# Feed-forward in three chunks of 768 tokens instead of four batches of 576, and a list schedule that no longer prefers the array shape in use

## The chip, the cores and the metric

The kernel runs on one core of one Trainium2 chip. The metric is the device time of one execution in microseconds (us); less is better. The engines are named as in the profile: PE is TensorE (matmuls), PEld its weight loads, DVE is VectorE, ACT is ScalarE, POOL is GpSimd, SP is SyncE, whose queue issues all the DMAs.

## The reference

Three layers follow one another on a batch of 4 with 576 tokens; the weights arrive as float64, the rest and the output are float32.

```python
# attention, 8 heads of 64, mask by blocks of 64 tokens
scores = scale * np.matmul(q, k.transpose(0, 1, 3, 2))
...
x = softmax(scores) @ v                      # (4, 576, 512)
# middle layer
theta = x @ w_theta
y = einsum('ts,bsd->btd', w_tok_r, x * cos(theta)) + einsum('ts,bsd->btd', w_tok_i, x * sin(theta))
u = x + y
x = u + np.maximum(u @ w_ch, 0.0)
# last layer
h = (x.transpose(0, 2, 1) @ U @ V).transpose(0, 2, 1)   # rank 32
u = x + h
out = u + np.maximum(u @ w_ch1, 0.0) @ w_ch2            # 512 -> 2048 -> 512
```

## The kernel before

**The whole program is planned on the host.** The code doesn't call the engines directly. It records every operation with a due time (`at_time`, `spread`, from the numbers in `CFG`), and `Line.run` then makes a list schedule: for each engine, in modelled time, it takes the ready operation with the lowest priority number (its due time, and in later rounds its latest start). `plan` repeats this `ROUNDS` times. The outcome is a fixed order of instructions on each engine; on the chip the engines wait for each other by semaphores alone. Tiles have tags, and a tag has homes (slots of SBUF or banks of PSUM); an operation whose tile finds no free home is passed over, and `LOOSE` says for which tags a later tile may overtake an earlier one.

**The choice on PE.** A matmul uses the array in a shape: 128 rows by 128 columns mostly, 64 by 128 for the scores (two heads at a time), 128 by 64 for the product with v. `Line.run` remembers the most urgent ready matmul, but if that one has another shape than the last one issued, it looks on, and takes the first one in its list that has the shape in use; only a candidate of a wrong shape ends the search, when it is due later than the first by more than `PATIENCE`, which is 0.

**Work in order.** 16 head pairs of attention (4 a batch); while they run, the weights of the middle layer are read and decoded from their float64 bits by ACT and DVE. Behind each four pairs comes the middle layer of that batch: `theta` (matmuls `th` of 512 columns), `sines`, `product`, `mix_r` and `mix_i` (token mix, tile `y`), `chan` (channel product, tile `c`), then `lowrank` and `expand`. `expand` writes u of the batch to DRAM (`u3d`). A matmul of float32 exactness is done as three matmuls of float32r parts: high with high, high with low, low with high (`three`, and loops like it).

**The feed-forward layer** takes the token columns of one batch in halves of 288 (`SH`), and uses a Strassen-Winograd scheme of 7 products for 2 by 2 blocks. Per batch and step j (8 steps of 256 hidden units):

- `make_u` reads u of the batch from `u3d` and splits it into two float32r parts (tile `uf`): for batch 1 into slots of the middle layer's `xT`, for the others into tag `U`.
- `ff1` makes four quarters of 12 matmuls (tile `m`, 288 columns), takes relu and the differences that the second product wants, seven pieces of h of 288 columns in all, and writes them to DRAM (`hd`) in four DMAs, three of them with two pieces.
- `ff2` reads them back (tile `hr`, tag `G`) in pairs of two pieces, splits them into float32r parts (tile `hv`, tag `U`, two pieces in one tile), and runs the products into eight PSUM banks (tile `acc`): s = 0 has four products, s = 1 three, each 2 x 3 matmuls. All eight steps j of s = 0 come first, then all of s = 1. `leave` then adds the banks and the residual u together (tiles `ea`, `eb`, `o`) and writes `outT`.

Tag `U` has 8 homes: four in SBUF space that attention gave up (`NU`), and four of the nine slots `T` that held the token weights. Tag `W` (weights w1 and w2 in parts) has the other five slots `T`, seven new ones (`NB`), and the slots of `w_theta` (`Kt`), `w_ch` (`Kc`) and U, V. A slot of `T` comes free for its second use when all tiles of that tag are done.

`EJ` is 5: the first five steps of batches 0 and 1 are due while the middle layer of batch 3 runs, the rest after it. The due times end with

```python
    late = [(b, j) for b in (0, 1) for j in range(EJ, NJ)] + [(b, j) for j in range(NJ) for b in (2, 3)]
    ...
    for b in range(B):
        for s in range(2):
            for j in range(NJ):
                at_time(t, ff2, b, s, j)
```

The operations are issued from one line at the very end of `build`, so nearly all rows of the profile carry that line, L1295; they are told apart by their tiles.

Of the kernel before, what the change touches and what calls it, by code (L numbers as in the profile page):

```python
# [45 lines left out]
CFG = dict(L=60., d0=0., d1=0.84, d2=1.0, dec=1.8, T=13.68, P=13.88, R=25.74, I=29.568, X=2.61, m0=4., m1=80., w1=1., w2=2., w3=0.2, u0=3., f1=150., f2=177., v0=0., v1=140.)  # L46
# [5 lines left out]
NB = 7  # L52
NRX = 5
NG = 7
NS_ = 4
INX = (1, 2, 6)
LONE = (2, 3)
NU = 4
UX = (1,)
EJ = 5  # L60
MIX = 0
NTW = 5
# [7 lines left out]
LOOSE = {"pm": 1, "pa": 1, "F": 3, "G": 6}  # L70
# [3 lines left out]
PATIENCE = 0.0  # L74
# [109 lines left out]
class Line:  # L184
# [143 lines left out]
    def fits(self, o):  # L328
        got = []
        for x in o.bufs:  # L330
            if x.home is not None or x.tag is None:
                continue
            free = [h for h in self.homes[x.tag] if h.since is not None and h not in [g for _, g in got]
                    and not any(self.left_of.get(a) for a in h.after[x.tag])]
            if not free:
                return None
            k = sum(y.tag == x.tag for y, _ in got)
            if x not in [y for _, _, y in self.order[x.tag][:k + 1]] and not len(free) > LOOSE.get(x.tag, 99):
                return None
            got.append((x, min(free, key=lambda h: h.since)))  # L340
        return got

    def run(self):
# [38 lines left out]
        while events:  # L382
# [18 lines left out]
            while c:  # L401
# [132 lines left out]
def build(tc, ctx, qT, kT, v, w_theta, wtokT, w_ch, U, V, w1, w2, outT):  # L534
# [38 lines left out]
    u3 = [dram.tile([DM, S], F32, name=f"u3d{b}") for b in range(B)]  # L573
    h3 = [[dram.tile([P, 7 * SH], F32, name=f"hd{b}_{j}") for j in range(NJ)] for b in range(B)]
# [60 lines left out]
    def abank(name):  # L635
        return line.tile([P, 512], F32, "pa", name, PSUM)

# [18 lines left out]
    u3d = [line.fixed(u, f"u3d{b}") for b, u in enumerate(u3)]  # L656
# [279 lines left out]
    def lowrank(b, i):  # L936
# [5 lines left out]
        xp = bank(f"xq{b}_{i}")  # L942
# [13 lines left out]
    def expand(b, d):  # L956
        gs_ = st[b]["Gs"]
        for g in range(2):
            gs = slice(g * SH, (g + 1) * SH)
            hp = bank(f"h{b}_{d}_{g}")  # L960
# [3 lines left out]
        nc.sync.dma_start(u3d[b][d * P:(d + 1) * P, :], xTs[b][:, d, 0:S])  # L964
# [34 lines left out]
    L = CFG["L"]  # L999
    for gp in range(NP):  # L1000
        spread(gp * L / NC4, (gp + 1) * L / NC4, pair_calls(gp))
# [5 lines left out]
    for b in range(B):  # L1007
        t0 = (b + 1) * L
# [15 lines left out]
    hd = [[line.fixed(h3[b][j], f"hd{b}_{j}") for j in range(NJ)] for b in range(B)]  # L1024
# [27 lines left out]

    def load_w1(f):
        t = line.tile([P, 2, DM], F32R, "W", f"w1_{f}")
# [9 lines left out]
    wparts, wv = {}, {}  # L1064

    def wpairs(j):
        q, k = divmod(j, 2)
        pair = [P, 2, 2, HW]
        if q in LONE:
            first = line.tile([P, 1, 2, HW], F32R, "W1", f"w2d{j}")  # L1070
        else:
            if q not in wparts:
                wparts[q] = line.tile(pair, F32R, "W", f"w2d{q}")
            first = wparts[q][:, k:k + 1]
# [31 lines left out]
    def make_u(b):  # L1106
        uu[b] = []
        for c in range(NC4):
            raw = rawslot(f"u3_{b}_{c}", F32)
            nc.sync.dma_start(raw, u3d[b][c * P:(c + 1) * P, :])  # L1110
            if b in UX:
                if c % 2 == 0:
                    x = xtile(f"uf{b}_{c}", [P, 2, 2, S], F32R)
                y = x[:, c % 2]
            else:
                y = line.tile([P, 2, S], F32R, "U", f"uf{b}_{c}")
            rnd("sh", y[:, 0], raw)
            sub(y[:, 1], raw, y[:, 0], "sl")
            uu[b].append(y)
# [4 lines left out]
    def fbank(name):  # L1124
        return line.tile([P, 512], F32, "F", name, PSUM)[:, :SH]
# [5 lines left out]
    def ff1(b, j):  # L1131
        n = f"{b}_{j}"
        ha, hb, hc, hdd = [halves(f"{x}{n}", tag="G") for x in ("ha", "hb", "hc", "hd")]

        def quarter(k, t):
            bank_ = fbank(f"m{n}_{k}{t}")
            w = w1t[2 * j + k]
            ts_ = slice(t * SH, (t + 1) * SH)
            for c in range(NC4):
                three(bank_, [w[g][:, c] for g in range(2)], [uu[b][c][:, g, ts_] for g in range(2)], c == 0, c == NC4 - 1)  # L1140
            return bank_

        relu(ha[:, 0], quarter(0, 0))
        relu(hc[:, 1], quarter(1, 1))
        m = quarter(0, 1)
        nc.vector.scalar_tensor_tensor(out=ha[:, 1], in0=m, scalar=0.0, in1=ha[:, 0], op0=ALU.max, op1=ALU.subtract)
        nc.sync.dma_start(hd[b][j][:, 0:2 * SH].rearrange("p (v c) -> p v c", v=2), ha)
        nc.vector.scalar_tensor_tensor(out=hb[:, 1], in0=m, scalar=0.0, in1=hc[:, 1], op0=ALU.max, op1=ALU.subtract)
        tt(hb[:, 0], hc[:, 1], ha[:, 1], ALU.subtract)
        nc.sync.dma_start(hd[b][j][:, 2 * SH:4 * SH].rearrange("p (v c) -> p v c", v=2), hb)  # L1150
        relu(hc[:, 0], quarter(1, 0))
        nc.sync.dma_start(hd[b][j][:, 4 * SH:6 * SH].rearrange("p (v c) -> p v c", v=2), hc)
        tt(hdd[:, 0], hc[:, 0], hb[:, 0], ALU.subtract)
        nc.sync.dma_start(hd[b][j][:, 6 * SH:], hdd[:, 0])
# [3 lines left out]
    def ff2(b, s, j):  # L1158
        w = wv[j]
        if s == 0:  # L1160
            group, at = FIRST4, ((0, 2, ("B11", "T1")), (2, 4, ("T2", "T3")))
        else:
            group, at = LAST3, ((4, 6, ("B21", "B22")), (6, 7, ("T4",)))
        v = {}
        for a, c, names in at:
            k = c - a
            raw = halves(f"hr{b}_{j}_{a}", n=k, tag="G")
            nc.sync.dma_start(raw, hd[b][j][:, a * SH:c * SH].rearrange("p (v c) -> p v c", v=k))
            t = line.tile([P, 2, 2, SH], F32R, "U", f"hv{b}_{j}_{a}")[:, :k]
            rnd("hh", t[:, :, 0], raw)  # L1170
            sub(t[:, :, 1], raw, t[:, :, 0])
            for i, x in enumerate(names):
                v[x] = t[:, i]
        for a, x, k in group:
            for m in range(2):
                if s == 0 and j == 0:
                    accs[b, k, m] = fbank(f"acc{b}_{k}_{m}")
                three(accs[b, k, m], [w[a][:, g, m * P:(m + 1) * P] for g in range(2)],
                      [x_ for x_ in (v[x][:, 0], v[x][:, 1])], s == 0 and j == 0, j == NJ - 1)
            if j == NJ - 1:  # L1180
                for m in range(2):
                    leave(b, s, k, m)

    def leave(b, s, k, m):
        if s == 0 and k == 0:
            r = [line.tile([P, S], F32, "G", f"o{b}_{2 * h + m}") for h in range(2)]
            for h in range(2):
                nc.sync.dma_start(r[h], u3d[b][(2 * h + m) * P:(2 * h + m + 1) * P, :])
            evs[b, m] = r, halves(f"ea{b}_{m}", tag="G"), halves(f"eb{b}_{m}", tag="G")
        r, ea, eb = evs[b, m]  # L1190
        acc = accs[b, k, m]
# [149 lines left out]
```

## Time and profile before

| | |
|---|---|
| median of 3 runs | 848.54 us (847.76 to 849.3) |
| the profiled execution | 847.5 us |
| its span in the profile | 845.7 us |
| busy: PE, PEld, DVE, ACT, POOL | 822.2, 740.3, 538.9, 451.1, 268.5 us |
| DMA traffic | 128.22 MB |

The span runs from the first to the last instruction of the profile, so 1.8 us of the execution lie around it. Busy time is the union of an engine's instructions; a matmul's row lasts longer than the distance to the next one (some 296 ns for 288 columns), since matmuls are pipelined. Prices of matmuls are therefore read from the starts of long runs.

### The profile page before, as it was taken

To read this page: it belongs to the slowest core of one execution; us is meant where nothing else is said; L and a number is where in the kernel's file an instruction comes from. 1 tells how busy PE (TensorE), PEld (TensorE's weight loads), DVE (VectorE), ACT (ScalarE), POOL (GpSimd) and SP (SyncE) were. 2 spreads that over 40 slices of the span, in tenths; PEclk is the share of its full clock that TensorE was granted. 3 is DMA by queue.
4 is the path that set the end of the run, shared out by engine and by line. 5 is a ranking of instruction groups with operands and counts; after the bars stand their busy time and mean duration, and the time that the engine had idled before them with its cause. 6 is when DMAs were issued, how large, how long until landed. Compare 5 with 4: busy or idle time off the path is not lost. (4 is left out here: it accounts for less than half of the span.)

```text
span 845.7 us, 16102 instructions
## 1 busy us (share of the span) xinstructions
PE 822.2 (97%) x5877; PEld 740.3 (88%) x5877; DVE 538.9 (64%) x1105; ACT 451.1 (53%) x1057; POOL 268.5 (32%) x323
## 2 busy tenths in 40 slices
PE   8998999999999999999999999999999999999997
PEld 6565678787888878988998999989999999999997
DVE  5999888747646475279734357466566566565653
ACT  6997888559635695357411234333444444444441
POOL 2345554443244441643303233322454010101010
PEclk9999999999999999999999999999999999999999
DMA  6554324210210102034442457679776868594831
GB/s 213 180 179 127 107 61 125 67 46 31 102 32 31 46 2 73 1 100 155 151 141 105 137 175 262 234 239 332 240 237 217 302 222 283 173 303 144 298 135 57
DMA packets 80464, 128.22 MB, mean 152 GB/s; under 512 B 8192, under 2 KB 34816, under 8 KB 80384
## 3 DMA queue, kind: packets, MB, share of 16 engines
q1 hardware_dynamic: 80384, 127.19, 45.3%
q8 instruction: 46, 0.75, 0.4%
q14 instruction: 34, 0.28, 0.1%
HBM read 84.69 MB, written 42.47 MB: 150 GB/s over the span
## 5 line engine op out<-in xcount | busy, mean ns | idle before, releaser
L1295 PE MATMUL m<-uf,w 128*128 128x288 f32 x1536 | 213.9, 296 | 0.7 <-POOL uf L1295 0.4
L1295 PEld LDWEIGHTS m<-uf,w 128*128 128x128 f32 x1536 | 207.1, 188 | 2.3 <-POOL uf L1295 0.9
L1295 ACT ACTIVATE hv<-hr 128x576 fp32r<-128x576 f32 x126 | 78.3, 624 | 96.0 <-PE acc L1295 80.6
L1295 DVE TENSOR_TENSOR hv<-hr,hv 128x576 fp32r<-128x576 f32 (+1 forms) x124 | 81.9, 688 | 67.2 <-ACT hv L1295 63.9
L1295 PE MATMUL y<-wtok,zh 128*128 128x288 f32 x576 | 120.9, 302 | 0.7 <-DVE xT L1295 0.6
L1295 ACT ACTIVATE P<-s,nm 128x128 f32<-128x128 f32 (+2 forms) x144 | 79.2, 554 | 37.7 <-DVE nm L1295 37.1
L1295 PEld LDWEIGHTS y<-wtok,zh 128*128 128x128 f32 x576 | 92.1, 188 | 4.4 <-DVE xT L1295 1.3
L1295 PE MATMUL y<-wtok,zl 128*128 128x288 f32 x288 | 84.8, 297 | 0.0
L1295 PE MATMUL t<-ident,P 128*128 128x128 f32 x400 | 63.3, 278 | 7.1 <-DVE PTA L1295 1.8
L1295 DVE TENSOR_REDUCE nm<-s 128x2 f32<-128x256 f32 (+4 forms) x80 | 63.8, 801 | 6.4 <-PE s L1295 3.1
L1295 DVE TENSOR_TENSOR xT<-y,xT 128x288 f32<-128x288 f32 x64 | 29.0, 456 | 59.0 <-PE y L1295 58.6
L1295 PE MATMUL s<-k,q 64*128 64x128 f32 (+4 forms) x320 | 64.3, 451 | 1.3 <-DMA k<-kT 1.2
L1295 PEld LDWEIGHTS t<-ident,P 128*128 128x128 f32 x400 | 46.6, 140 | 21.6 <-ACT PTB L1295 4.2
L1295 PE MATMUL acc<-hv,w2c 128*128 128x288 f32 x384 | 61.7, 296 | 2.2 <-DVE o L1295 2.2
L1295 PE MATMUL c<-u,wch 128*128 128x288 f32 x384 | 59.3, 301 | 0.9 <-DVE xT L1295 0.4
L1295 PEld LDWEIGHTS acc<-hv,w2c 128*128 128x128 f32 x384 | 54.3, 188 | 3.2 <-DVE o L1295 3.2
L1295 PEld LDWEIGHTS c<-u,wch 128*128 128x128 f32 x384 | 53.2, 189 | 4.3 <-issue 1.3
L1295 POOL TENSOR_TENSOR o<-o,ea 128x288 f32<-128x288 f32 x8 | 6.3, 812 | 151.2 <-DVE ea L1295 151.2
L1295 PEld LDWEIGHTS y<-wtok,zl 128*128 128x128 f32 x288 | 53.8, 188 | 0.3
L1295 PE MATMUL th<-wth,xh 128*128 128x512 f32 x160 | 50.8, 399 | 1.2 <-DVE f L1295 1.1
L1295 POOL TENSOR_TENSOR hb<-hc,ha 128x288 f32<-128x288 f32 x24 | 19.8, 826 | 81.9 <-DVE ha L1295 45.4
L1295 ACT ACTIVATE hc<-m 128x288 f32<-128x288 f32 x49 | 19.9, 408 | 47.2 <-PE m L1295 43.5
(212 smaller groups left out, 1567.0 us busy)
## 6 DMA issues: line engine op xcount, KB each, us to landing
hr<-hd SPq DMA_DIRECT2D x96, 288.0 KB, 4.7
hd<-hc SPq DMA_DIRECT2D x32, 288.0 KB, 2.6
hd<-ha SPq DMA_DIRECT2D x32, 288.0 KB, 2.3
hd<-hb SPq DMA_DIRECT2D x32, 288.0 KB, 2.4
raw_w<-w SPq DMA_DIRECT2D x32, 256.0 KB, 2.8
w2raw<-w SPq DMA_DIRECT2D x32, 256.0 KB, 4.1
raw_tok<-wtokT SPq DMA_DIRECT2D x18, 288.0 KB, 2.9
q<-qT SPq DMA_DIRECT2D x16, 320.0 KB, 3.0
```

The costliest lines, as they stand in the source:

```text
L1295: fn(*[place(x) for x in args], **{k: place(x) for k, x in kw.items()})
```

## The change

The token columns of the feed-forward layer, 2304 in all, are cut into three chunks of 768 (`NCK`, `CT`) in halves of 384 (`TH`), across the borders of the batches. `ff1` now keeps six pieces of h, one DMA each; the seventh, T4, is made again in `ff2` by a subtraction. `ff2` reads a piece into the third part of the tile it is split in (tile `hv`, tag `U`), without a slot of its own; only the raw copy for T4 has one (tag `raw`).

Slots move with it. All nine slots `T` go to tag `U`; chunk 0's u sits in six new slots (`U0`), of which one turns into `U` and five into `W` afterwards; chunk 1's u sits in `U`, chunk 2's in `U` and one slot of `xT`. `LOC1` says for each of the 16 parts of w1 where it goes and when it is due: B new slots, K the slots of `w_theta`, X slots of `xT`, C the slots of `w_ch`, which come free after the last channel matmul (parts 13 to 15, of steps 6 and 7). Early due are now the eight steps of chunk 0, then (`late`) the first five of chunk 1, the first five of chunk 2, and the rest in turn. The residual u is read (`residual`) before step 5 of s = 0, not in the last one.

In `Line.run`, the search for a matmul of the shape in use now ends at the first candidate, of whatever shape, that is due more than `CFG["pat"]`, 1779.728 ns, after the most urgent one. All due times in `CFG` are set anew.

```diff
-CFG = dict(L=60., d0=0., d1=0.84, d2=1.0, dec=1.8, T=13.68, P=13.88, R=25.74, I=29.568, X=2.61, m0=4., m1=80., w1=1., w2=2., w3=0.2, u0=3., f1=150., f2=177., v0=0., v1=140.)
+CFG = dict(pat=1779.728, L=60, p1=8.002, q1=121.819, q2=240, M0=56.95, ML=60, u1=8, d0=0, d1=0.605, d2=1, dec=2.205, T=11.455, P=8.796, R=29.254, I=29.614, X=3.64, m0=12.498, m1=66.907, w1=1.927, w2=4.193, w3=0.209, wx=33.959, u0=13.081, f1=171.125, f2=179.274, v0=-4.697, v1=130.895)
...
-NB = 7
+NB = 5
 NRX = 5
-NG = 7
-NS_ = 4
-INX = (1, 2, 6)
-LONE = (2, 3)
-NU = 4
-UX = (1,)
-EJ = 5
-MIX = 0
-NTW = 5
+NG = 2
+NS_ = 8
+INX = (2, 6, 7)
+LOC1 = "XXBBBBBKKKKXXCCC"
+NCK = 3
+E1 = 5
+EB = "pm"
+CT = NT // NCK
+TH = CT // 2
+NU = 6
...
                 if got is None:
                     stash.append(item)
+                elif o is not None and item[0][0] > o.prio[0] + CFG["pat"]:
+                    stash.append(item)
+                    break
                 elif e != PE_ or way.mode == mode:
                     o, take = x, got
                     break
                 elif o is None:
                     o, take = x, got
                     stash.append(item)
-                elif item[0][0] > o.prio[0] + PATIENCE:
-                    stash.append(item)
-                    break
                 else:
                     stash.append(item)
...
-            late = {"RT": {"G": ("RT",)}, "T": {"W" if i < NTW else "U": ("T",)}}.get(tag, {})
+            late = {"RT": {"G": ("RT",)}, "T": {"U": ("T",)}}.get(tag, {})
...
-    for tag, n in {"U": NU, "W": NB, "G": NRX}.items():
+    for tag, n in {"U0": NU, "W": NB, "G": NRX}.items():
         for i in range(n):
-            line.home("w1p", f"{tag}e{i}", **{tag: ALL})
+            then = {"U" if i == 0 else "W": ALL + ("U0",)} if tag == "U0" else {}
+            line.home("w1p", f"{tag}e{i}", **{tag: ALL}, **then)
...
+    def ff2(n, s, j):
         w = wv[j]
...
+        group = LAST3 if s else FIRST4
         v = {}
...
+        for a, x, k in group:
+            t = v[x] = line.tile([P, 3, TH], F32R, "U", f"hv{n}_{j}_{x}")
+            if x == "T4":
+                raw = single(f"hr{n}_{j}", "raw")
+                nc.sync.dma_start(raw, hcols(n, j, "T2"))
+                tt(raw, f32(v["B21"][:, 2]), raw, ALU.subtract)
+            else:
+                raw = f32(t[:, 2])
+                nc.sync.dma_start(raw, hcols(n, j, x))
+            rnd("hh", t[:, 0], raw)
+            sub(t[:, 1], raw, t[:, 0])
...
+    late = [(1, j) for j in range(E1)] + [(2, j) for j in range(E1)] + [(n, j) for j in range(E1, NJ) for n in (1, 2)]
+    for i, (n, j) in enumerate(late):
+        at_time(t + CFG["f1"] * i / len(late), ff1, n, j)
...
+    step = CFG["f2"] / NCK / NJ / 7
+    for n in range(NCK):
         for s in range(2):
             for j in range(NJ):
-                at_time(t, ff2, b, s, j)
+                if s == 0 and j == NJ - 3:
+                    at_time(t, residual, n)
+                at_time(t, ff2, n, s, j)
                 t += step * (3 if s else 4)
```

## Rows read from the trace of the kernel before

**Rows 1.** The page, part 1: an engine, busy us (share of the span), instructions.

```profile
PE 822.2 (97%) x5877; PEld 740.3 (88%) x5877; DVE 538.9 (64%) x1105; ACT 451.1 (53%) x1057; POOL 268.5 (32%) x323
```

**Rows 2.** Busy us by stretch: PE, PEld, DVE, ACT, POOL; granted clock, DMA share, GB/s.

```profile
0.00:140.00 140.00, 128.98 (x884) 94.70 (x885) 119.92 (x264) 117.53 (x326) 65.93 (x77) 1.00 0.46 144
140.00:360.00 220.00, 218.91 (x1522) 181.59 (x1522) 129.44 (x268) 135.53 (x331) 86.66 (x108) 1.00 0.14 45
360.00:500.00 140.00, 136.86 (x964) 130.14 (x963) 82.44 (x177) 53.23 (x117) 43.33 (x53) 1.00 0.40 132
500.00:564.00 64.00, 63.01 (x459) 60.85 (x458) 41.22 (x88) 25.04 (x58) 22.04 (x28) 1.00 0.69 237
564.00:659.00 95.00, 94.76 (x715) 94.52 (x714) 57.84 (x124) 41.21 (x99) 39.56 (x47) 1.00 0.77 264
659.00:842.00 183.00, 179.69 (x1343) 178.52 (x1342) 108.07 (x187) 78.52 (x130) 11.00 (x13) 1.00 0.63 211
```

**Rows 3.** The chain that ended last, in order of time: start us, us, what.

```profile
569.64 6.98 DMA u<-u3d
...
577.42 81.41 PE m L1295 x612
...
687.09 42.04 PE acc L1295 x314
...
729.17 0.45 DVE eb L1295
...
774.69 0.45 DVE eb L1295
```

**Rows 4.** PE timeline, 676 to 692 us: start us, us, instruction, count, [idle before].

```profile
687.09 1.07 PE L1295 MATMUL acc<-hv,w2c 128*128 128x288 f32 x6 [0.59 <-DVE o L1295]
```

**Rows 5.** PE timeline, 62 to 90 us.

```profile
70.86 0.74 PE L1295 MATMUL th<-wth,xh 128*128 128x512 f32 x2
71.44 0.40 PE L1295 MATMUL th<-wth,xl 128*128 128x512 f32 x1
...
73.53 0.40 PE L1295 MATMUL th<-wth,xl 128*128 128x512 f32 x1
```

**Rows 6.** PE timeline, 380 to 384 us.

```profile
380.74 0.39 PE L1295 MATMUL th<-wth,xl 128*128 128x512 f32 x1
...
382.80 0.39 PE L1295 MATMUL th<-wth,xl 128*128 128x512 f32 x1
```

**Rows 7.** ACT groups by form: out<-in, form, count | busy us, mean ns | idle before.

```profile
L1295 ACT ACTIVATE hv<-hr 128x576 fp32r<-128x576 f32 x94 | 64.0, 685 | 87.2 <-PE acc L1295 76.2 <-DMA hr<-hd 6.4 <-PE m L1295 1.7
...
L1295 ACT ACTIVATE hv<-hr 128x288 fp32r<-128x288 f32 x32 | 14.3, 446 | 8.8 <-PE acc L1295 4.4 <-DMA hr<-hd 1.5
```

**Rows 8.** DVE groups by form, columns as in the group above.

```profile
L1295 DVE TENSOR_TENSOR hv<-hr,hv 128x576 fp32r<-128x576 f32 x96 | 71.4, 757 | 67.2 <-ACT hv L1295 63.9 <-DMA hr<-hd 2.5
...
L1295 DVE TENSOR_TENSOR hv<-hr,hv 128x288 fp32r<-128x288 f32 x28 | 12.7, 452 | 0.0
```

**Rows 9.** Tile hr (h read back): ns of an issue, and landing, min/median/max.

```profile
L1295 SPq DMA_DIRECT2D hr<-hd x128: 319/377/1126, 505.2 to 818.9; - x128
...
DMA to landing us min/median/max: 2.6/4.6/6.4
```

**Rows 10.** DMA issues: tile, queue, count, KB each, median us to landing.

```profile
hd<-ha SPq DMA_DIRECT2D x32, 288.0 KB, 2.3
...
hd<-hd SPq DMA_DIRECT2D x32, 144.0 KB, 2.7
```

**Rows 11.** First-product matmuls (tile m) by stretch, PE busy us.

```profile
360.00:500.00 140.00, 61.79 (x419) 1.00 0.40 132
```

**Rows 12.** Token-mix matmuls (tile y) by stretch, PE busy us.

```profile
500.00:564.00 64.00, 0.00 (x0) 1.00 0.69 237
```

**Rows 13.** PE timeline, 60 to 66 us.

```profile
62.16 0.73 PE L1295 MATMUL th<-wth,xh 128*128 128x512 f32 x2
...
64.44 0.61 PE L1295 MATMUL th<-wth,xh 128*128 128x512 f32 x2
```

More of the change, by code (lines that the diff above doesn't have):

```diff
@@ L337, in fits @@
             k = sum(y.tag == x.tag for y, _ in got)
-            if x not in [y for _, _, y in self.order[x.tag][:k + 1]] and not len(free) > LOOSE.get(x.tag, 99):
+            if x not in [y for _, _, y in self.order[x.tag][:k + 1]] and not len(free) > LOOSE.get(x.name[:1] + x.tag, LOOSE.get(x.tag, 99)):
                 return None
@@ L636, in abank, with ebank @@
         return line.tile([P, 512], F32, "pa", name, PSUM)
+    def ebank(name):
+        return line.tile([P, 512], F32, EB, name, PSUM)
     def wtile(name, tag):
@@ L654, in xtile @@
         return line.tile(shape, dt, "xT", name)
-    u3d = [line.fixed(u, f"u3d{b}") for b, u in enumerate(u3)]
+    u3d = line.fixed(u3, "u3d")
     xTs = {}
@@ L1023, in build @@
         spread(t0, t0 + CFG["X"], [(expand, b, d) for d in range(NC4)])
-    hd = [[line.fixed(h3[b][j], f"hd{b}_{j}") for j in range(NJ)] for b in range(B)]
+    hd = [[line.fixed(h3[n][j], f"hd{n}_{j}") for j in range(NJ)] for n in range(NCK)]
     def tt(out, a, b, op):
@@ L1062, in load_w1 @@
         sub(t[:, 1], f32(d), t[:, 0], "dl")
-    wparts, wv = {}, {}
+    wv = {}
     def wpairs(j):
-        q, k = divmod(j, 2)
         pair = [P, 2, 2, HW]
[L1069 to L1074, printed above, removed]
+        first = line.tile([P, 1, 2, HW], F32R, "W1", f"w2d{j}")
         if j in INX:
@@ L1104, in build, with make_u, piece @@
     uu = {}
[L1106 to L1119, printed above, removed]
+    def make_u(n):
+        free, made = [], 0
+        def piece():
+            nonlocal made
+            if not free:
+                tag = ("U0", "U", "U")[n]
+                if n == 2 and made == 3:
+                    x = xtile("ux", [P, 6, TH], F32R)
+                    free.extend(x[:, i] for i in range(6))
+                else:
+                    x = line.tile([P, 3, TH], F32R, tag, f"uf{n}_{made}")
+                    free.extend(x[:, i] for i in range(3))
+                made += 1
+            return free.pop(0)
+        uu[n] = {}
+        for t in range(2):
+            for c in range(NC4):
+                raw = single(f"u3_{n}_{c}{t}", "raw")
+                a = n * CT + t * TH
+                nc.sync.dma_start(raw, u3d[c * P:(c + 1) * P, a:a + TH])
+                h, l = uu[n][c, t] = piece(), piece()
+                rnd("sh", h, raw)
+                sub(l, raw, h, "sl")
     FIRST4 = (("A11", "B11", 0), ("S2", "T2", 1), ("S3", "T3", 2), ("S1", "T1", 3))
@@ L1124, in fbank @@
     def fbank(name):
[L1125 removed]
+        return line.tile([P, 512], F32, "F", name, PSUM)[:, :TH]
     def three(bank_, w, u, start, stop):
@@ L1176, in ff2, with places, residual, leave @@
                 if s == 0 and j == 0:
[L1177 to L1179 removed]
+                    accs[n, k, m] = fbank(f"acc{n}_{k}_{m}")
+                three(accs[n, k, m], [w[a][:, g, m * P:(m + 1) * P] for g in range(2)],
+                      (v[x][:, 0], v[x][:, 1]), s == 0 and j == 0, j == NJ - 1)
             if j == NJ - 1:
                 for m in range(2):
[L1182 to L1186, printed above, removed]
[L1187 to L1193 removed]
+                    leave(n, s, k, m)
+    def places(n, m):
+        return ([slice((2 * h + m) * P, (2 * h + m + 1) * P) for h in range(2)],
+                [slice(n * CT + t * TH, n * CT + (t + 1) * TH) for t in range(2)])
+    def residual(n):
+        for m in range(2):
+            rows, cols = places(n, m)
+            r = {}
+            for h in range(2):
+                for t in range(2):
+                    r[h, t] = single(f"o{n}_{m}{h}{t}", "G")
+                    nc.sync.dma_start(r[h, t], u3d[rows[h], cols[t]])
+            evs[n, m] = r, [single(f"e{n}_{m}{i}", "G") for i in range(3)]
+    def leave(n, s, k, m):
+        rows, cols = places(n, m)
+        r, (s1, u2, u3) = evs[n, m]
+        acc = accs[n, k, m]
+        def out(h, t):
+            nc.sync.dma_start(outT[rows[h], cols[t]], r[h, t])
         if s == 0:
```

141 lines of the change are left out of this document (69 added, 72 removed).

## The prediction, made before the changed kernel ran

> **What bounds the kernel now.** I read the page first: TensorE (PE) is busy 97% of the span [rows 1]. A busy PE need not be a full one, so I cut the span into stretches at the points where the work changes [rows 2]: attention alone with the weight decoding (0 to 140 us), attention beside the middle layer (to 360), the middle layer of the last batches with early feed-forward work (to 500), the low-rank step with feed-forward work (to 564), first feed-forward product alone (to 659), second product (to 842). PE's idle time by stretch is 11.0, 1.1, 3.1, 1.0, 0.2 and 3.3 us. The granted clock reads 1.00 in all of them, the 2.4 GHz level. So PE sets the time everywhere; only in the first 140 us do VectorE (DVE, 119.9 of 140 us busy) and ScalarE (ACT, 117.5) press on it. From 564 us on there is hardly anything to win but the cost of the matmuls themselves.
>
> The chain that ended last says the same: from 577 us it is one run of matmuls, broken once per batch by DVE work on the accumulators [rows 3]. In the PE timeline that break costs PE 0.59 us of idle time [rows 4].
>
> **The price of a matmul.** 612 matmuls of 288 columns took 81.41 us, 133.0 ns each [rows 3]. The second product repeats every 45.52 us (774.69 less 729.17) for 8 x 7 x 2 x 3 = 336 matmuls; less the 0.59 us of idle time that is 133.7 ns each [rows 3, 4]. The trace before has no matmul of 384 columns in this data type; the nearest on the other side has 512. There the third of each triple starts at 71.44 and at 73.53 us, nine matmuls apart: 232 ns each; a later run (380.74 to 382.80) gives 229 [rows 5, 6]. I take 230.5. On the line from 288 to 512, 384 columns cost 133.0 + 96 x (230.5 - 133.0) / 224 = 174.8 ns, for the second product 175.5. Bounds from both neighbours: if time went as the columns alone, 133.0 x 4/3 = 177.3 from below and 230.5 x 3/4 = 172.9 from above.
>
> The Trainium skill, "TensorE: Matmul & The Clock Gate", section "Back-to-back issue gap", has a warm matmul cost its columns at 2.4 GHz and 2.5 ns more: 122.5 ns for 288. The trace has 133.0, so the rule lacks some 10 ns here. With its small fixed part the 2160 new matmuls would save only 1.8 us on the 2880 old ones (351.0 against 352.8 us), as an estimate from that page.
>
> **Part 1: three chunks of 768 tokens.** First product: 1536 x 133.0 ns = 204.3 us becomes 3 x 8 x 48 = 1152 x 174.8 ns = 201.4 us: -2.9 us (bounds -5.1 and 0). Second product: 4 x 45.52 = 182.1 us becomes 3 x (336 x 175.5 ns + 0.7 us break) = 179.0 us: -3.1 us (bounds -5 and 0). The break grows with the columns of the DVE adds, hence 0.7, but there are three. Together -6.0 us. That is small because the columns stay the same in number, 442,368 in the first product; only the fixed part of a matmul is saved 720 times.
>
> The other engines get work in other shapes. Each piece of h is now rounded (ACT) and subtracted (DVE) alone, at 384 columns. On the lines between the 288 and 576 forms, ACT needs 446 + 239/3 = 526 ns, DVE 452 + 305/3 = 554 ns [rows 7, 8]. 168 pieces and 24 subtractions for T4, which is no longer stored, make DVE 106 us instead of 84 us, and ACT 88 us instead of 78. DVE was busy 108.1 of 183 us in this stage [rows 2]; 130 of 177 still lies under PE, 74%. Nothing on the path; if that cover were gone, it would be 22 us.
>
> h's DMAs go from 128 written and 128 read to 144 and 168, of 192 KB. An issue takes SP's queue 0.38 us [rows 9], so 56 more cost it 21 us out of the 340 us of feed-forward work. Landing doesn't hang on size: 2.7 us for 144 KB, 2.3 for 288 KB [rows 10]. I take nothing. So too for the new places of the weights, the one array for u, the residual read that starts three steps ahead of the break and the stores of 192 KB at the end: the engines and the DMAs that do this run under PE here (DMA share 0.63 to 0.77 [rows 2]), and if the residual read came late, one break per chunk would grow by its landing.
>
> **Part 2: pieces of h are read straight into the tile they are split in.** Before, second-product operands sat in 8 tiles of two pieces, with raw copies in other slots read still further ahead. Now there are 10 tiles (nine of the token weights' and one more), a piece each, and the DMA waits for a free one. PE uses a piece in 6 x 175.5 ns = 1.05 us, so a tile comes round every 10.5 us. Its cycle: landing 4.6 us (2.6 to 6.4) [rows 9], ACT 0.53, DVE 0.55, PE 1.05, together 6.7 us, 8.5 at the longest landing. Covered by 2 to 4 us, with SP's in-order queue between: a DMA that waits for its tile holds back residual loads and output stores behind it. I cost it at nothing; the first rival is that it isn't.
>
> **Part 3: early feed-forward work.** Between 360 and 500 us PE filled the middle layer's waits with 61.8 us of first-product matmuls [rows 11], of two batches with five steps each. Now only chunk 0 has its operands there: chunk 1's go into the token weights' tiles, free after the last token mix (no such matmul stands after 500 us [rows 12]). Of chunk 0's eight steps, the last two need weights that wait for the slots of the last channel matmuls. Six steps are 6 x 48 x 174.8 ns = 50.3 us, so 11.5 us less to fill with. This costs from nothing (the middle layer just runs denser, and PE is 98% busy there) to 11.5 us. I take 1: the stretch lost only 3.1 us of 140 to waits.
>
> After 564 us the wait for the last batch's u (6.98 us of DMA on the chain [rows 3]) was covered by other batches' steps; now chunk 1's first five (42 us) cover it.
>
> **Part 4: the order.** A ready matmul of the shape in the array used to go first, however late its turn; now only if it is due within 1.78 us of the most urgent one. What that costs is shape switches. After a group of 64-row score matmuls the first two of 512 columns take 0.73 or 0.74 us, where a pair within a run takes 0.61 [rows 5, 13]: 0.11 us or a little more a switch. A head pair has three score groups and two value groups in other shapes, so at most 10 switches; if all were merged into two runs before it had 4. 16 pairs x 6 x 0.11 = 10.6 us is the worst.
>
> The Trainium skill speaks against this part: "TensorEngine Tiling (Array Packing)", section "Key Properties", says that changing the tiling mode drains TensorE. The 0.11 us agree in kind; the page has no price.
>
> What it may win is idle time: 15.2 us before 500 us, 11.0 of them in the first 140. There the score matmuls feed the softmax on DVE and ACT, and the new times spread the weight decoding over 132 us instead of 108 (60 x 2.205 against 60 x 1.8). Both act at the right place, but DVE at 86% and ACT at 84% leave limited room. Bounds: from -15.2 to +10.6 us. I take -5: under half of the 11.0 us, switches already paid. This is the least supported term.
>
> **Sum.** The profiled execution took 847.5 us (845.7 span and 1.8 around it): 847.5 - 2.9 - 3.1 + 1 - 5 = 837.5. The median of the runs shown, 848.5, is 1.0 us above that execution; half of that added gives 838.
>
> **Rivals.**
> - A, second product starves. Place: 659 us to the end. If a tile's cycle passes 10.5 us by x, PE loses x/10 per piece, 168 pieces: 16.8 us for 1 us. It eats the whole gain from x = 0.6. For it: tiles hold one piece where they held two, and nothing is read ahead of them. Against: 6.7 us of cycle, DMA share 0.63 in this stage. At x = 1: 855.
> - B, feed-forward runs short between 360 and 500 us. All 11.5 us missing become idle and the new order wins nothing: 847.5 - 6.0 + 11.5 = 853. For it: ACT is 38% and DVE 59% busy there, so PE's dependents are latency chains, which need filling. Against: batch 2's middle layer fills too.
> - C, the order wins most of the early idle time: -12 us instead of -5, 831 or less.
> - D, the change gives nothing: the cost of a matmul goes as its columns (177.3 ns for 384), and the switches cancel what urgent matmuls win: 847 to 849. For it: 512 columns would then cost 236 ns, and the trace has up to 232. Against: 229 in the later run. The Trainium skill's page on the clock gate, with its small fixed part, lies near this case.
>
> **How the numbers follow.** Forecast 0.58, on its own 832 to 846 (bounds of the columns, and half of those of the order); A 0.08, B 0.10, C 0.12, D 0.12. 0.2%, 1.7 us, is about what can be told from no change. Faster takes the forecast, C and a little of D: 0.71; same is most of D: 0.10; slower is A, B and a rest: 0.19. 829 to 851 leaves out A, half of B and the far part of C, 0.18.
>
> **What would show it.** A run of first-product matmuls at 173 to 177 ns each, 2160 in all feed-forward work; a period of 59 to 60 us for a chunk's second product, with one break near 0.7 us and no idle time put down to ACT or DVE pieces or the h reads; PE idle in the first 140 us below 11 us; PE idle from 360 to 500 us near 3 us. Wrong, if PE waits for pieces of h after the first product (A), shows gaps ahead of middle-layer matmuls (B), or if pairs of the early matmuls carry the 0.11 us far more often without less idle time.

## The result, and the profile after

The changed kernel takes 835.36 us (median of four runs, 834.85 to 838.07) against 848.92 us before: ratio 0.9846, interval 0.9819 to 0.9872. It is 13.6 us faster; 838 was predicted. The profiled execution is the slowest of the four, 838.07 us with a span of 836.3, so its rows account for 9.4 us against the 847.5 of the profiled execution before.

First the page's line of busy times, then the stretches of [rows 2], columns as there.

```profile
PE 812.7 (97%) x5131; PEld 729.0 (87%) x5131; DVE 537.8 (64%) x1086; ACT 418.7 (50%) x1015; POOL 330.5 (40%) x404
```

```profile
0.00:140.00 140.00, 127.07 (x854) 90.41 (x854) 114.49 (x250) 115.98 (x318) 65.85 (x78) 1.00 0.46 142
140.00:360.00 220.00, 219.58 (x1533) 181.62 (x1532) 136.28 (x284) 140.49 (x346) 92.55 (x116) 1.00 0.16 51
360.00:500.00 140.00, 137.87 (x883) 132.40 (x882) 76.89 (x159) 53.01 (x112) 45.56 (x51) 1.00 0.39 125
500.00:564.00 64.00, 63.52 (x366) 61.99 (x365) 39.46 (x81) 29.38 (x73) 25.22 (x29) 1.00 0.69 230
564.00:659.00 95.00, 95.00 (x548) 95.00 (x547) 48.06 (x90) 35.48 (x82) 41.96 (x45) 1.00 0.70 226
659.00:836.00 177.00, 169.70 (x958) 167.54 (x956) 122.59 (x225) 44.38 (x87) 59.39 (x86) 0.99 0.71 218
```

PE's idle time is 12.9, 0.4, 2.1, 0.5, 0.0 and 7.3 us by stretch (the last one holds the tail after the last matmul). Against [rows 2] it grew in the first 140 us, where the prediction looked for the gain, by 1.9 us; it fell by 2.2 us in the next three. First-product matmuls from 360 to 500 us, to be held against [rows 11]:

```profile
360.00:500.00 140.00, 62.25 (x321) 1.00 0.39 125
```

The chain, to be held against [rows 3] (start us, us, what):

```profile
528.15 122.09 PE m L1344 x702
650.24 4.96 PE acc L1344 x29
...
745.10 1.02 DVE e L1344 x2
...
804.73 1.01 DVE e L1344 x2
```

702 matmuls of 384 columns took 122.09 us: 173.9 ns each. On the chain the second product follows at 650.24 us; before, it followed at 658.83 (577.42 + 81.41). So 8.6 of the 9.4 us are won ahead of it: 4.0 by the columns (204.3 us before, 1152 x 173.9 ns = 200.3 now), 4.6 by something else. The program cut at the second product's first matmul and at its last, columns as above, first before, then now:

```profile
0.00:658.68 658.68, 642.20 (x4534) 561.49 (x4534) 430.73 (x918) 372.21 (x928) 257.20 (x311) 1.00 0.41 134
658.68:840.93 182.25, 180.01 (x1346) 178.84 (x1344) 107.70 (x186) 78.84 (x131) 11.32 (x13) 1.00 0.63 211
```

```profile
0.00:650.08 650.08, 634.11 (x4123) 552.50 (x4124) 409.53 (x855) 371.86 (x923) 266.49 (x315) 1.00 0.39 127
650.08:832.46 182.38, 178.62 (x1009) 176.46 (x1008) 127.54 (x231) 46.86 (x92) 64.05 (x90) 0.99 0.72 220
```

Ahead of the second product PE's idle time is 16.5 us before and 16.0 now, so nearly all of the 8.6 us are busy time, not waiting. The second product itself wins nothing, 182.4 us against 182.2; the 0.8 us behind 650.24 lie after its last matmul. The period from the second chunk to the third is 59.63 us (804.73 less 745.10), as predicted; the first chunk is another matter. Two views of its break, between the four products and the three: PE's timeline, and the clock around it (stretches as above).

```profile
687.93 0.80 PE L1344 MATMUL acc<-hv_T,w2a 128*128 128x384 f32 x3 [2.12 <-DVE e L1344]
...
689.61 2.12 PE L1344 MATMUL acc<-hv_B,w2c 128*128 128x384 f32 x6
```

```profile
688.00:690.00 2.00, 2.00 (x9) 1.98 (x10) 2.00 (x5) 1.05 (x2) 0.00 (x0) 0.70 0.95 317
690.00:692.00 2.00, 2.00 (x8) 2.00 (x7) 2.00 (x5) 0.94 (x2) 0.00 (x0) 0.50 0.96 318
692.00:694.00 2.00, 2.00 (x13) 2.00 (x12) 2.00 (x6) 0.53 (x1) 0.00 (x0) 0.94 0.72 203
```

PE sat idle for 2.12 us (0.59 in [rows 4]), and then six matmuls lasted 2.12 us where six take 1.20 elsewhere: the granted clock had fallen to 0.50, the 1.2 GHz level.

### The profile page after: what moved, and what is told of

Same layout as the page of the kernel before. It is cut to its first block, busy times and chain, and to the rows that moved or that the text cites. A ratio compares the mean times of both kernels' runs of the same rounds, so it can differ in the third digit from the quotient of the medians.

```text
span 836.3 us, 14804 instructions
## 1 busy us (share of the span) xinstructions
PE 812.7 (97%) x5131; PEld 729.0 (87%) x5131; DVE 537.8 (64%) x1086; ACT 418.7 (50%) x1015; POOL 330.5 (40%) x404
## 4 chain that ended last, share of the span: by engine, by line
PE 85%; DVE 8%; DMA 3%; ACT 2%; issue 1%; SPq 0%; POOL 0%; DVEq 0%; POOLq 0%; ACTq 0%
PE m L1344 23%; PE acc L1344 18%; PE y L1344 14%; PE th L1344 7%; PE c L1344 6%; PE s L1344 5%; PE t L1344 4%; PE oB L1344 3%; DVE o L1344 1%; PE G L1344 1%; PE oA L1344 1%; ACT P L1344 1%; DMA hv_T<-hd 1%; DVE da_tok L1344 1%; PE xq L1344 1%
## 5 line engine op out<-in xcount | busy, mean ns | idle before, releaser
L1344 PE MATMUL m<-uf,w 128*128 128x384 f32 x756 | 144.6, 337 | 0.0
L1344 PEld LDWEIGHTS m<-uf,w 128*128 128x128 f32 x756 | 131.8, 188 | 0.7 <-issue 0.4
L1344 ACT ACTIVATE P<-s,nm 128x256 f32<-128x256 f32 (+3 forms) x144 | 78.9, 552 | 40.9 <-DVE nm L1344 36.4
L1344 ACT ACTIVATE hB<-m 128x384 f32<-128x384 f32 x60 | 28.8, 488 | 89.1 <-PE m L1344 84.1
L1344 ACT ACTIVATE hv_B<-hv_B 128x384 fp32r<-128x384 f32 x40 | 20.8, 525 | 83.1 <-DMA hv_B<-hd 77.0
L1344 DVE TENSOR_TENSOR hv_T<-hv_T 128x384 fp32r<-128x384 f32 x68 | 42.0, 634 | 30.9 <-POOL hv_T L1344 24.2
L1344 DVE SCALAR_TENSOR_TENSOR hT<-m,hB 128x384 f32<-128x384 f32 x48 | 25.0, 551 | 53.6 <-PE m L1344 42.3
L1344 PE MATMUL m<-uf,wx 128*128 128x384 f32 x252 | 51.3, 339 | 0.0
L1344 DVE TENSOR_TENSOR hv_B<-hv_B 128x384 fp32r<-128x384 f32 x67 | 38.3, 584 | 15.6 <-POOL hv_B L1344 14.0
L1344 POOL TENSOR_SCALAR hv_B<-hv_B 128x384 fp32r<-128x384 f32 x30 | 19.6, 652 | 70.3 <-DMA hv_B<-hd 40.4
```

The lines of the kernel that those rows point to most:

```text
L1344: fn(*[place(x) for x in args], **{k: place(x) for k, x in kw.items()})
```

## The experiments

All times are medians of five or more runs, or of four where that is said; ratios are against runs of the kernel before on the same chip, whose median was 849.73, 848.56 and 849.39 us for the three sets of four. These lie 1.2 us apart, so a difference in us between two sets, or to the 835.36 us above, is good to about 1 us only. After the result I had three theories. Theory 1: columns some 7 us, the new order the rest, rule and due times alike. Theory 2: the rule gives what the columns don't. Theory 3: a list schedule's outcome scatters with any change of its numbers, and the new numbers are a good draw.

**1. The changed kernel with the old rule on PE.**

```diff
-                elif o is not None and item[0][0] > o.prio[0] + CFG["pat"]:
-                    stash.append(item)
-                    break
                 elif e != PE_ or way.mode == mode:
...
+                elif item[0][0] > o.prio[0] + 0.0:
+                    stash.append(item)
+                    break
```

> The changed kernel with the old choice on PE (a ready matmul of the shape in use goes first, patience 0), all else as changed. Theory 1 (the feed-forward columns give some 7 us of the 13.6, the new order the rest, by rule and times about equally): 838 to 840 us. Theory 2 (the rule alone gives the part that the columns don't): 841 to 843 us, with the idle time of PE before 500 us back near 15 us. Theory 3 (the new numbers are just a good draw, and any change of the plan costs some us): 837 to 846, and as much when a due time that has nothing to do with the rule is moved a little.

853.11 us, ratio 1.0041 (1.0025 to 1.0056): slower than the kernel before, 18 us behind the changed one. No theory had so much. PE's timeline shows where (start us, us, instruction, count, idle before):

```profile
514.90 0.40 PE L1344 MATMUL G<-x2l,UVst 128*128 128x512 f32 x1
515.13 4.53 PE L1344 MATMUL m<-uf,w 128*128 128x384 f32 x25
...
523.86 35.57 PE L1344 MATMUL m<-uf,w 128*128 128x384 f32 x204
...
571.75 10.57 PE L1344 MATMUL m<-uf,w 128*128 128x384 f32 x60
582.16 0.60 PE L1344 MATMUL xq<-ident,xT 128*64 128x128 f32 x4
583.43 0.50 PE L1344 MATMUL G<-x2h,UVst 64*128 64x512 f32 x1 [0.67 <-ACT x2h L1344]
...
586.04 0.53 PE L1344 MATMUL h<-UVst,Gs 128*128 128x288 f32 x2 [1.39 <-DVE Gs L1344]
...
594.45 1.01 PE L1344 MATMUL m<-uf,wx 128*128 128x384 f32 x2 [4.17 <-POOL uf L1344]
```

The low-rank step of batch 3 is done up to its last 64 tokens at 515 us. The transposes of these (`xq`, 128 by 64) and their two matmuls (`G`, 64 by 128) have another shape than the rest, and wait while 67 us of first-product matmuls go by, all that are in stock. Then the stock is empty, and the chain transposes, `G`, `h`, write of u, read, split runs with PE bare: 4.17 us of idle time at its end, and the clock goes down with it (the stretch from 590 to 600 us: granted clock 0.50, the 1.2 GHz level):

```profile
590.00:600.00 10.00, 5.83 (x18) 5.55 (x18) 4.51 (x9) 3.55 (x7) 0.51 (x1) 0.50 0.89 282
```

**2. The kernel before with the new rule.** The edit is the reverse of the first, with a patience of 1779.728 ns.

> The kernel before with the new choice on PE alone (matmuls of the shape in use only if due within 1.78 us of the most urgent). Theory 1: 846 to 848 us. Theory 2: 842 to 844 us. Theory 3: 847 to 856, since the old due times were set for the old rule.

849.62 us, ratio 1.0001 (0.9992 to 1.0011). The rule alone gives nothing in four batches with the old times, but that is the sum of three differences between the profiled executions. The last group of the value product, the end of attention, starts at 362.08 us instead of 352.55, 9.5 later. From there to the second product it takes 5.5 us less (the last transposes of 64 tokens move ahead, from 554 us to 523). And the second product takes 3.3 us less, since this plan has no breaks in it. What delays attention comes with experiment 3.

**3. The changed kernel with the old due times ahead of the feed-forward part.**

```diff
-CFG = dict(pat=1779.728, L=60, p1=8.002, q1=121.819, q2=240, M0=56.95, ML=60, u1=8, d0=0, d1=0.605, d2=1, dec=2.205, T=11.455, P=8.796, R=29.254, I=29.614, X=3.64, m0=12.498, m1=66.907, w1=1.927, w2=4.193, w3=0.209, wx=33.959, u0=13.081, f1=171.125, f2=179.274, v0=-4.697, v1=130.895)
+CFG = dict(pat=1779.728, L=60., p1=8., q1=120., q2=240., M0=60., ML=60., u1=8, d0=0., d1=0.84, d2=1.0, dec=1.8, T=13.68, P=13.88, R=25.74, I=29.568, X=2.61, m0=12.498, m1=66.907, w1=1.927, w2=4.193, w3=0.209, wx=33.959, u0=13.081, f1=171.125, f2=179.274, v0=-4.697, v1=130.895)
```

> The changed kernel with the due times of attention, weight decoding and middle layer as before (60 us a batch), the rule and the feed-forward part as changed. Theory 1: 838 to 840 us. Theory 2: 835 to 837. Theory 3: 837 to 846.

847.69 us, ratio 0.9978 (0.9963 to 0.9993): 12 us lost. The last group of the value product shows the most of it. In PE's timeline it starts at 354.44 us in the changed kernel,

```profile
354.44 2.22 PE L1344 MATMUL oB<-PTB,vr 128*64 128x320 f32 x20
```

and here at 364.36:

```profile
364.36 2.27 PE L1344 MATMUL oB<-PTB,vr 128*64 128x320 f32 x20
```

The profiled execution is 5.3 us above the median here, so the others need not have all of these 10 us. Two things make them up. Until that group PE is idle for 17.9 us, against 13.4 in the changed kernel: 4.5 more. And behind the longest of its pauses the granted clock falls to the lower level:

```profile
107.44 0.52 PE L1344 MATMUL t<-ident,P 128*128 128x128 f32 x3 [2.51 <-POOL P L1344]
```

```profile
100.00:110.00 10.00, 5.96 (x42) 4.25 (x41) 7.60 (x21) 9.46 (x21) 6.76 (x8) 0.94 0.56 190
110.00:120.00 10.00, 8.25 (x39) 5.65 (x39) 7.86 (x16) 9.69 (x19) 5.73 (x5) 0.54 0.08 26
```

A clock of 0.94 and 0.54 over 10 us each costs at most 0.6 + 4.6 = 5.2 us. The second experiment, with the same rule and times, has the same pause of 2.51 us at 106.58 and a clock of 0.82 and 0.67 in these stretches. It isn't one execution: the mean granted clock is 0.989 to 0.993 in the twelve of this version and 0.990 to 0.994 in the twelve of experiment 2, against 0.995 to 0.998 in the four of the changed kernel. So under the new rule the new due times spare the kernel this pause, and some of the 12 us are what the clock costs behind it.

**4. The kernel before with the new due times ahead of the feed-forward part.** The edit is the reverse of the third, with `pair_at` and `moe_at` put in.

> The kernel before with the new due times of attention, weight decoding and middle layer, its rule and feed-forward part unchanged. Theory 1: 846 to 848 us. Theory 2: 848 to 850. Theory 3: 847 to 856.

854.68 us, ratio 1.0063 (1.0042 to 1.0085). Under the old rule the new times harm. Here the last transposes of 64 tokens start at 585.86 us, 62.58 us of first-product matmuls go by on the chain before that, and PE idles for 3.0 us behind them, much as in experiment 1. The profiled execution is 6.9 us longer than before: 4.5 us up to the last value group, 5.6 from there to the second product, less 3.2 by a second product without breaks. So theories 1 and 2 fall in this form: neither the rule nor the times have a worth of their own. Theory 3's ranges hold two of the four numbers (experiments 2 and 4), and it says nothing about the 67 us of waiting in the first run. I set a fourth against it: the old rule's harm in three chunks is that one step, and little else.

**5. The changed kernel with the old rule, but that one step freed.** The six instructions are booked as 128 by 128 in the plan, so that they are never passed over for their shape; what runs on the chip is the same.

```diff
+            o.mode = (128, 128) if self.plain else (k, m)
...
+        line.plain = b == B - 1 and i == 4
```

> The changed kernel with the old rule on PE, except that the four transposes and two matmuls of the last 64 tokens of batch 3's low-rank step count as having the 128 by 128 shape, so that they need no right of way. Theory 4, formed on the first four runs (the old rule's harm is that this one step waits behind every ready first-product matmul, from 514 to 582 us in that run, until the stock is empty): these matmuls stand near 520 us, and the time falls from 853 to between 831 and 837. Theory 3 (any change of the plan is a new draw, and the published numbers are a good one): 840 to 853.

840.96 us, ratio 0.9908 (0.9896 to 0.9920). 12.2 of the 17.8 us come back. The time misses theory 4's range and lies at the lower end of theory 3's, so it is the place that decides: of the 11.8 us between the two profiled executions 11.5 lie between the last value group and the second product. That is the mechanism of theory 4, and most of its size. The 5.6 us that stay away are not one place: the second product starts 2 to 4 us later than in two profiles of the new rule (652.08 us against 650.08, and 648.09 in experiment 8) and takes up to 2.3 us longer. PE's timeline has the transposes at 519.89 us, where the first experiment had 582.16:

```profile
519.89 0.60 PE L1347 MATMUL xq<-ident,xT 128*64 128x128 f32 x4
```

**6. The kernel before, that one step freed.** Same edit.

> The kernel before with its own rule, the same six instructions of batch 3's low-rank step counted as 128 by 128. Theory 4: they move from about 555 us to 520 or 530, the time falls by 2 to 5 us, to 845 to 848, less than in three chunks, since four batches leave more first-product work in stock. Theory 3: 848 to 855.

846.21 us, ratio 0.9968 (0.9956 to 0.9980): 2.7 us by the ratio, in theory 4's range, but not by its mechanism. The transposes go from 554 us to 516, and yet the stretch from the last value group to the second product, in which they lie, gets no shorter; first before, then here:

```profile
352.55:658.68 306.13, 301.77 (x2185) 291.30 (x2181) 181.83 (x388) 122.98 (x281) 111.93 (x135) 1.00 0.57 191
```

```profile
352.86:660.94 308.08, 302.46 (x2184) 291.56 (x2181) 184.84 (x384) 126.27 (x289) 115.43 (x132) 1.00 0.56 190
```

What got shorter is the second product: 178.9 us instead of 182.2, one run in the chain with no break:

```profile
661.10 177.59 PE acc L1298 x1335
```

On DVE two of the additions that free no bank (`o<-o,ea`, at 688.90 and 689.94 us around the first break) now stand behind those that do (`o<-acc,o`, 687.50); before, they stood ahead of them (683.97 and 686.60). These 3.3 us are more than the whole gain. So no run shows that the wait of the last 64 tokens costs the kernel before anything: PE has other matmuls to run meanwhile (1.0 us idle from 500 to 564 us [rows 2]). That theory 4's range was hit is luck.

**7. The changed kernel with three additions moved behind the break.**

```diff
             if k == 0:
                 nc.scalar.copy(s1, acc)
             elif k == 1:
                 tt(u2, acc, s1, ALU.add)
-                tt(r[0, 1], r[0, 1], u2, ALU.add)
-                tt(r[1, 0], r[1, 0], u2, ALU.add)
             elif k == 2:
                 tt(u3, acc, u2, ALU.add)
-                tt(r[1, 1], r[1, 1], u3, ALU.add)
             else:
                 tt(r[1, 1], acc, r[1, 1], ALU.add)
-                out(1, 1)
...
+                if s == 1 and j == 2:
+                    at_time(t, settle, n)
```

`settle` holds the three additions and the store.

> The changed kernel with the three additions into the residual that read no PSUM bank (and the store after one of them) due three steps later, so that the additions that free a bank of the second product come first on DVE. If the break between the first four and the last three products is DVE's order, PE's idle time there goes from 2.9, 0.7 and 0.7 us to under 0.3 each, and the time to 830 to 834. If the banks are late for another reason (the pieces of h or the residual's DMA), it stays at 834 to 837. Theory 3: 836 to 846.

831.11 us (four runs), ratio 0.9791 (0.9774 to 0.9808), 4.3 us ahead of the changed kernel and the fastest version here, with the twelfth. (The first break's idle time was 2.12 us in the changed kernel, not 2.9.) DVE's timeline around the first break, of the changed kernel and of this one (e and o are the sums and the residual; `e<-acc,e` and `o<-acc,o` free a bank, `o<-o,e` doesn't):

```profile
683.89 1.01 DVE L1344 TENSOR_TENSOR e<-acc,e 128x384 f32<-128x384 f32 x2
684.82 2.59 DVE L1344 TENSOR_TENSOR o<-o,e 128x384 f32<-128x384 f32 x3
687.33 0.55 DVE L1344 TENSOR_TENSOR e<-acc,e 128x384 f32<-128x384 f32 x1
687.80 1.01 DVE L1344 TENSOR_TENSOR o<-o,e 128x384 f32<-128x384 f32 x2
688.73 1.01 DVE L1344 TENSOR_TENSOR o<-acc,o 128x384 f32<-128x384 f32 x2
```

```profile
680.50 1.94 DVE L1351 TENSOR_TENSOR e<-acc,e 128x384 f32<-128x384 f32 x4
682.36 1.01 DVE L1351 TENSOR_TENSOR o<-acc,o 128x384 f32<-128x384 f32 x2
```

In the changed kernel 2.59 us of `o<-o,e` stand in front of the last `e<-acc,e`, for which PE waits. Moved away, the whole second product is one run in the chain:

```profile
648.51 175.68 PE acc L1351 x1006
```

175.68 us for 1006 of its 1008 matmuls, 174.6 ns each: no break is left. Up to the first break PE runs the same matmuls in the same order as in the changed kernel, so this is the cleanest of the experiments.

**8. The changed kernel with one due time moved a little** (`R=29.254` to `R=29.3`).

> The changed kernel with one due time moved by a hair (the length of mix_r, 29.254 to 29.3 us). Theories 1 and 4: 833 to 838. Theory 3 (draw): 838 to 850.

835.14 us (four runs), ratio 0.9839 (0.9826 to 0.9851). The plan changed in a few places of the middle layer only, so this is a weak test of theory 3; it serves better as a second profile of nearly the same plan. There PE's idle time from 360 to 500 us is 0.4 us, and the 2.05 us at the first break did not bring the clock down, so the 838.07 us of the profiled execution hold some 3 us that are not the plan's.

**9. The kernel before with new rule and new times together.** Experiments 2 and 4 in one.

> The kernel before, four batches, with both the new rule and the new due times of attention, weight decoding and middle layer: what is left against the changed kernel is the three chunks alone. Theory 1 (the chunks give their columns' 7 us, less the 3 that their breaks lose): 839 to 842 us. If the chunks give nothing by themselves: 834 to 837. Theory 3 (each change of the plan is a draw of its own): 845 to 855.

843.81 us, ratio 0.9948 (0.9931 to 0.9966). Between theory 1 and 3: the three chunks alone are worth 8.4 us under the new order. 6.8 us are columns: 4.0 in the first product as above; in the second, a run without breaks of 1344 x 133 ns = 178.8 us against 176. Here it is such a run:

```profile
663.36 177.59 PE acc L1303 x1335
```

The breaks of the changed kernel take 4.3 us of that back (experiment 7), so some 5.9 us come from elsewhere (8.4 - 6.8 + 4.3). Between 360 and 564 us PE is idle for 6.1 us here and for 2.6 in the changed kernel, but this profiled execution, 848.71 us, is 4.9 above the median of its version, with a granted clock of 0.98 and 0.97 in these stretches. How much of the 5.9 us belongs to three chunks as such stays open. Of the 5.6 us that rule and times together win in four batches, the vanished breaks are 3.3.

**10. The changed kernel with the old due times of the weight decoding alone** (`d1=0.84, d2=1.0, dec=1.8`).

> The changed kernel with the old due times of the weight decoding alone (ends at 108 us instead of 132). The step of the prediction that spread decoding relieves DVE in the first 140 us: 839 to 843 us, and attention ends 3 us or more later than at 356. If the attention's and the middle layer's own times did it: 834 to 837.

835.82 us (four runs), ratio 0.9839 (0.9821 to 0.9858). No difference, and the last value group starts at 353.70 us, no later than in the changed kernel: spread decoding wins nothing.

**11. The changed kernel with the patience at 0** (`pat=0.`).

> The changed kernel with the patience at 0: a matmul of the shape in use goes first only at the same due time as the most urgent one. If shape switches cost 0.11 us each and that is all: some 20 to 40 switches more in attention, 837 to 840 us. If the order of attention hangs on a little right of way: 841 to 848. If 1.78 us is no better than none: 834 to 837.

841.48 us, ratio 0.9910 (0.9894 to 0.9927): 6.1 us lost, just inside the range of the second expectation; the first counted on fewer switches. Counted over neighbouring matmuls in the trace, the array's shape changes 173 times up to the end of attention, against 120 in the changed kernel and 104 before. The last value group starts at 360.19 us, 5.75 us later than at 354.44: 0.11 us for each of the 53 more. But PE is also idle for less of that time, with the same work done; first the changed kernel up to that group, then this one:

```profile
0.00:354.44 354.44, 341.09 (x2340) 267.33 (x2341) 250.31 (x532) 253.51 (x657) 152.99 (x188) 1.00 0.28 88
```

```profile
0.00:360.19 360.19, 349.25 (x2338) 267.00 (x2338) 248.72 (x545) 252.64 (x652) 147.96 (x182) 1.00 0.28 86
```

Its busy time grew by 8.2 us, 0.15 us a switch, of which 2.4 us took the place of waiting.

**12. Version 7 with five of the ten tiles for pieces of h held.** Tiles of tag `U` are taken by a small memset at the third step and to be let go by another at the end.

> The changed kernel with the additions after the break (831.1 us), and five of the ten tiles for pieces of h held by two small memsets each from the third step of the second product to its end, so that a tile comes round every 5.2 us instead of 10.5. By the measured landing (2.7 to 3.4 us) a tile's cycle is 0.53 + 0.56 + 1.05 more, 4.8 to 5.5 us and waits on top: PE loses 0 to 0.15 us per piece, 831 to 855 us. By the cycle of the prediction, 6.7 us: 0.3 us per piece, some 45 us more, 875. If a tile's number doesn't matter: 831.

830.06 us (four runs), ratio 0.9791 (0.9765 to 0.9817). The experiment did not do what it was made for: the second memsets had nothing to wait for, so the plan put all ten together, before the second product, and the tiles were free again.

```profile
L1361 DVE MEMSET held<- x10: 59/59/59, 647.3 to 648.2; 128x1 f32 x10
```

It is a repeat of version 7, and the number of tiles stays untested.

The versions that differ in three things alone, medians in us; the last three columns are of the profiled execution: where the last value group starts, from there to the second product, and the second product from its first matmul to the end of its last.

| feed-forward | rule | due times ahead of it | us | ratio to before | value group | to second product | second product |
|---|---|---|---|---|---|---|---|
| four batches | old | old | 848.6 to 849.7 | 1 | 352.6 | 306.1 | 182.2 |
| four batches | new | old | 849.6 | 1.0001 | 362.1 | 300.6 | 178.9 |
| four batches | old | new | 854.7 | 1.0063 | 357.1 | 311.7 | 179.1 |
| four batches | new | new | 843.8 | 0.9948 | 355.1 | 308.1 | 178.9 |
| three chunks | new | old | 847.7 | 0.9978 | 364.4 | 300.6 | 182.4 |
| three chunks | old | new | 853.1 | 1.0041 | 355.7 | 308.3 | 182.8 |
| three chunks | new | new | 835.4 | 0.9846 | 354.4 | 295.6 | 182.4 |

The corner of three chunks with old rule and old times was not run.

## Why the prediction was right, and which of its steps were not

- **Price of 384 columns: right.** 174.8 and 175.5 ns predicted from its neighbours; 173.9 in the first product, 174.6 in the second without breaks. First product -4.0 us instead of -2.9. So rival D, 177.3 ns, didn't come. The Trainium skill's rule for an isolated warm matmul in "TensorE: Matmul & The Clock Gate", section "Back-to-back issue gap", would have 162.5 ns, as an estimate; the trace has 11 ns more, as it had before.
- **Second product: the term for the breaks was too small.** 179.0 us predicted with 0.7 us a break, 3.1 less than before; in the profiled execution it took 182.4 us, no less than before. Two breaks were 0.7 us; the first was 2.12 and cost clock besides. Experiment 7 shows the cause, DVE's order, and what all breaks cost: 4.3 us of the median. The prediction sized the break by the columns of DVE's additions and took their order as given.
- **Rival A didn't come.** PE's waits in the second product name a piece of h once, for 0.2 us; the rest is the breaks:

```profile
PE acc L1344 <- DVE e L1344: 2.1, 1, 2.1
...
PE acc L1344 <- DVE o L1344: 1.5, 2, 0.7
...
PE acc L1344 <- DVE hv_T L1344: 0.2, 1, 0.2
```

Landing was shorter than [rows 9] had it: 3.4 us at the median for T pieces, 2.7 for B pieces. Whether fewer tiles would starve PE is open. The other engines didn't press either: POOL took part of the pieces (59.4 us from 659 us on, 11.0 before), and DVE was busy for 122.6 of 177 us there.

- **Rival B didn't come, and Part 3 was wrong in its sign.** From 360 to 500 us PE had 62.25 us of first-product matmuls, as much as before: 321 matmuls are 6.7 steps, where the prediction counted on six. The shortage that B feared is real in three chunks, but it comes when the last step waits (experiment 1), not for lack of weights.
- **Part 4 is the step that failed, though its sum held.** The prediction took -5 us (with Part 3's +1: -4), and what isn't columns gave 4.6 ahead of the second product. But it took them as idle time won in the first 140 us, through score matmuls and spread decoding. There PE's idle time rose to 12.9 us, ahead of the second product it fell by 0.5 us in all, and experiment 10 shows the decoding worth nothing. What fell is PE's busy time behind attention; in which matmuls, beyond the columns, no run shows. That the size came out is luck; rival C, -12 us of idle time, didn't come. The runs showed a step that was overlooked: the last 64 tokens of a low-rank step use the array in other shapes, and right of way held them back behind all the first-product work. In three chunks that costs 12 us of 18 (experiment 5), which the new rule avoids; it isn't a gain on the kernel before, where freeing the step won nothing ahead of the second product (experiment 6).
- **The price of a switch: right in size, a little low.** 0.11 us or a little more predicted (the rows that it reads give 0.12 and 0.13); experiment 11's 53 more switches put the end of attention back by 0.11 us each and PE's busy time up by 0.15. The new order has 16 more than before, some 1.8 to 2.5 us, of the 10.6 that were the worst case.
- **What stays open.** The due times ahead of the feed-forward part are worth 12 us under the new rule. Up to the end of attention more idle time and the clock behind a pause can account for it (experiment 3), though why the old times have that pause is not shown; the rest, between attention and the second product, is open. It isn't the decoding. Theory 3 is not refuted for this part: the times may be a good draw among many, though experiments 8 and 10 changed them and lost nothing. The sum of -10 us was thus right partly for wrong reasons: the first product gave more than predicted, the second nothing, and the rest came where it was not looked for.

## What to carry to other kernels

A scheduler that prefers what is cheap next must bound that preference: free, it let one tiny step wait behind all the filler there was (67 us, and some 12 of them in the end time in three chunks; in the kernel before, where the filler lasted, nothing that shows); at none, it paid 53 switches of 0.11 to 0.15 us. Look for the rare shape at the end of a chain, not only for the frequent ones. Where an engine both frees a bank and does sums that nobody waits for, the former goes first: moving three additions won a third as much as the whole change, and the four-batch plan of experiment 6, with that order, has 3.3 us less in its second product. A gain in an experiment counts for a theory only if it lies where the theory puts it.

## What the runs showed of the hardware

A pause of PE of 2.12 us in otherwise dense matmuls was followed by a granted clock of 0.50 in one execution (0.70 from 688 to 690 us, 0.50 to 692, 0.94 to 694). In another, of nearly the same plan, the clock stayed at 1.00 behind a pause of 2.05 us (experiment 8). A pause of 2.51 us in attention, where PE was less dense, was followed by a granted clock of 0.94 from 100 to 110 us and 0.54 to 120 (experiment 3). So the price of a break isn't its idle time alone, and one kernel's executions can differ by it. A switch of the array's shape cost 0.11 us of time and 0.15 us of PE's busy time, over 53 of them at once.
